# Attention and a gated feed-forward layer on one core: the weight scale from column sums for six steps and from squares for twelve

## The chip, the cores and the metric

The kernel runs on one core of a Trainium2 chip. The metric is device microseconds (us) of one execution. The five engines are named as the profile names them: PE (matrix products), DVE (VectorE), ACT (ScalarE), POOL (GpSimd) and SP (which mostly issues DMAs). Each takes the instructions of its own queue strictly in order.

## The reference

Eight batches of eight heads of causal attention (576 positions, 64 columns) with a bias from cumulative sums, and behind it a gated feed-forward layer over all 4608 positions:

```python
scores = q @ k.T / sqrt(64)
bias   = -(cum[:, None] - cum[None, :])            # cum: running sum of max(s, 0)
scores = where(causal, -1e9, scores + minimum(bias, 0))
attn   = softmax(scores)
x      = (attn @ v)  as  [4608, 512]
gate   = sigmoid(x @ w_gate);  val = x @ w_val     # 512 -> 1536
out    = (gate * val) @ w_out                      # 1536 -> 512
```

All inputs are float32 values held in 64-bit floats; the outputs have to be as accurate as float32 products.

## The kernel before

Products run as sums of float16 products: each operand is scaled by a power of two and split into a high part and a low part, and three of the four part products are added. The first eight heads (NN = 8) are an exception: they are computed in float32 (functions whose names begin with n_), and their instructions are emitted inside `first()`, which raises their priority by 1000 in the scheduler.

The program is emitted in ticks, five to a head (NTL = 5, one for each block of query rows). A tick emits scores (line 489 and 491), masked maxima (529), exponentials (530), the split of the probabilities (534, 539) and the products with v (562 to 564) of neighbouring heads, and, from tick 44 on (NE), units of the feed-forward layer. A unit (g, f) takes 256 positions and 128 of the 1536 hidden columns: `ffn_in` (24 products at line 714, tanh at 719, the gate at 721), `ffn_mid` (the split of the hidden values, 729 and 730) and `ffn_out` (products at 744). The first two groups, g = 0 and 1, run all 24 of their `ffn_in` first, then `hidden_scale`, which needs the scales of all weights, and only then their `ffn_out`.

The weights come in 18 steps. Steps 0 to 11 each bring 128 columns of w_gate and w_val, steps 12 to 17 each 256 rows of w_out. A step is `load_weight` (DMA, lines 279 and 286, most of them issued from ACT's queue), `decode_weight` (64-bit to 32-bit: one ACT and three DVE operations on 128x1024, lines 298 to 301), the scale, and `split_weight` (high part on ACT, line 337, low part on DVE, line 338). The rooms into which raw and decoded weights go are borrowed: ws and wa are their own, w2all is the future w_out, t2f the gates of the first two groups, io the output rows. Step n can be loaded when the step that last used its room is through. Steps 0 to 5 are emitted in ticks below 40, during the float32 heads; steps 6 to 17 from tick 44 on, by `emit_unit`'s neighbours in the loop, so that a unit's weights are ready three units ahead.

For the scale, `column_bound` multiplies the upper 16 bits of the decoded magnitudes (read as bfloat16) by a matrix of ones: eight products at line 310 into one bank, a maximum over them on DVE (313), and two small integer operations (332, 334) that make a power of two of it. The else branch for weights that aren't 64-bit (`m is None`) exists already and isn't used: a Square with a running sum on ACT (326), a sum over the partitions on POOL (328), and the two small operations of `pow2_of` (148, 150).

The order on each engine is set when the program is built: a scheduler takes the emitted instructions, their dependences, priorities and modelled costs and writes down one sequence for each engine. `keep_in_program_order` pins a few loads.

Of the kernel before, what the change touches and what calls it, by code (L numbers as in the profile page):

```python
# [10 lines left out]
F32 = mybir.dt.float32  # L11
F32R = mybir.dt.float32r
I32 = mybir.dt.int32
I64 = mybir.dt.int64
AF = mybir.ActivationFunctionType
ALU = mybir.AluOpType
ADD_REDUCE = bass.bass_isa.ReduceOp.add

P = 128
# [6 lines left out]
def tile_attention_then_gated_ffn(  # L26
# [11 lines left out]
    nc = tc.nc  # L38
# [11 lines left out]
    NTL = len(TILES)  # L50
# [4 lines left out]
    NN = H  # L55
# [7 lines left out]
    pp = ctx.enter_context(tc.tile_pool(name="pp", bufs=2, space=bass.MemoryType.PSUM))  # L63
# [69 lines left out]
    wscale = cp.tile([P, 2, NF], F32, name="wscale")  # L133
# [8 lines left out]
    def first(now=True):  # L142
        return tc.high_priority(1000) if now else ExitStack()

    def pow2_of(dst, ss, tag):

        e = wp.tile([P, 1], I32, tag="xe", name=f"xe_{tag}")
        nc.vector.tensor_scalar(e, ss.bitcast(I32), 1, 0x3F800000, ALU.logical_shift_right, ALU.bitwise_and)
        n = dst.shape[1]
        nc.vector.tensor_scalar(dst.bitcast(I32), e.to_broadcast([P, n]) if n > 1 else e, -1.0, 204.0 * 2.0 ** 23,  # L150
                                ALU.mult, ALU.add)
# [72 lines left out]

    wide = w_gate.dtype == I64
    wst, wdec, wtot = {}, {}, {}

    rows_out = cp.tile([P, 2 * DM], F32, name="io")
    t2big = cp.tile([P, 2 * NF * GT], F32, name="t2f")
# [23 lines left out]
    def room(n):  # L253

        o, f = wsteps[n]
        if o == 0:
            return raw[f % 3], dec[f % 3], n - 3
        i, j, last = outroom[f // 2]
        return raw[i], dec[j], last
# [30 lines left out]
    def decode_weight(n):  # L290

        o, f = wsteps[n]
        r, a, _ = room(n)
        if not wide:
            return a.bitcast(F32), None
        m = w2all[:, f // 2].rearrange("p l h x n -> p (l h x n)") if o else w1[f].rearrange("p c g l n -> p (c g l n)")
        m = m.bitcast(I32)
        nc.scalar.activation(a.bitcast(F32), r[:, :, 1].bitcast(F32), AF.Copy, scale=2.0 ** -112)
        nc.vector.tensor_scalar(m, a, 3, 0x7FFFFFF8, ALU.logical_shift_left, ALU.bitwise_and)
        nc.vector.scalar_tensor_tensor(a, a, -0x80000000, m, ALU.bitwise_and, ALU.bitwise_or)  # L300
        nc.vector.scalar_tensor_tensor(a, r[:, :, 0], 29, a, ALU.logical_shift_right, ALU.bitwise_or)
        return a.bitcast(F32), m

    def column_bound(n, m):

        top = m.bitcast(BF16).rearrange("p (n t) -> p n t", t=2)[:, :, 1]
        early = wnext["tick"] < NTL * NN
        ps = pp.tile([P, 512], F32, tag="av" if early else "o", name=f"wps{n}", **({"bufs": 1} if early else {}))
        for c in range(8):
            nc.tensor.matmul(ps[:, :P], ones, top[:, c * P : (c + 1) * P], start=c == 0, stop=c == 7)  # L310
        tot = wp.tile([P, 1], F32, tag="wst", name=f"wtot{n}")
        junk = lp.tile([P, P], BF16, tag="wj", name=f"wj{n}")
        nc.vector.tensor_scalar(junk, ps[:, :P], 2.0 ** -100, None, ALU.max, ALU.max, accum_out=tot)
        return tot

    def split_weight(n, a, m):

        o, f = wsteps[n]
        if o:
            hi, lo = (w2all[:, f // 2, l].rearrange("p h x n -> p (h x n)") for l in range(2))  # L320
        else:
            a = a.rearrange("p (c n) -> p c n", n=P)
            hi, lo = (w1[f].rearrange("p c g l n -> p (c g) l n")[:, :, l] for l in range(2))
        if m is None:
            ss = wp.tile([P, 1], F32, tag="wss", name=f"wss{n}")
            nc.scalar.activation(hi, a, AF.Square, accum_out=ss)
            tot = wp.tile([P, 1], F32, tag="wst", name=f"wtot{n}")
            nc.gpsimd.partition_all_reduce(tot, ss, P, ADD_REDUCE)
            pow2_of(wscale[:, o, f : f + 1 + o], tot, f"w{n}")
        else:  # L330
            e = wp.tile([P, 1], I32, tag="xe", name=f"xe_w{n}")
            nc.vector.tensor_scalar(e, column_bound(n, m).bitcast(I32), 0x7F800000, None, ALU.bitwise_and)
            dst = wscale[:, o, f : f + 1 + o]
            nc.vector.tensor_scalar(dst.bitcast(I32), e.to_broadcast([P, 2]) if o else e, -1.0, 268.0 * 2.0 ** 23,
                                    ALU.mult, ALU.add)
        sc = wscale[:, o, f : f + 1]
        nc.scalar.activation(hi, a, AF.Copy, scale=sc)
        nc.vector.scalar_tensor_tensor(lo, a, sc, hi, ALU.mult, ALU.subtract)
# [21 lines left out]
        osc[b] = wp.tile([P, 1], F32, tag="osc", name=f"osc{b}", bufs=3)  # L360
        nc.vector.tensor_scalar(osc[b], gmax, sv[b][1], 2.0 ** 14, ALU.mult, ALU.mult)

    wnext = {"load": 0, "step": 0, "tick": 0}

    def weight_step():
        n = wnext["step"]
        while n and wnext["load"] < len(wsteps) and room(wnext["load"])[2] < n:
            if not NF <= wnext["load"] < NF + 2:
                load_weight(wnext["load"])
            wnext["load"] += 1  # L370
        split_weight(n, *decode_weight(n))
        wnext["step"] = n + 1
# [426 lines left out]
    for n in range(nticks + 12):  # L799
        if n == NTL * EARLY:  # L800
            more_room()
        i, t = divmod(n, NTL)
        wnext["tick"] = n
        if i < NN:
            with first():
                n_s(i, NTL - 1 - t)
# [7 lines left out]
        if 2 <= n < nticks + 2:  # L814
            a, z = divmod(n - 2, NTL)
# [5 lines left out]
        if 1 <= n < nticks + 1:  # L821
            a, z = divmod(n - 1, NTL)
# [7 lines left out]
        if 3 <= n < 3 + NTL * NN:  # L830
            with first():
                a, z = divmod(n - 3, NTL)
# [113 lines left out]
        if n >= NE and state["u"] < 2 * NF:  # L946
            fdone = min(NF, int((n - NE + 1) * FPT))
            while state["u"] < 2 * fdone:
                f = state["u"]
# [17 lines left out]
        m = n - (11 if n > 2 * NTL * H + 30 else 7)  # L967
# [42 lines left out]
```

## Time and profile before

| | |
|---|---|
| median of 3 runs | 1151.53 us (1150.67 to 1153.77) |
| profiled execution, its own time | 1150.28 us |
| its span | 1148.5 us |
| granted TensorE clock, mean | 0.993 |
| PE busy | 1096.8 us, 96% |
| DVE, ACT, POOL busy | 756.4, 733.5, 199.9 us |

All durations below are from the one profiled execution; the time outside its span is 1.78 us. Rows of the profile name line, engine, operation, output <- input and the shape; a row that begins with a number gives start and duration in us, and in square brackets how long the engine had been idle before it and what it waited for. A table by windows gives for each stretch its length, each engine's busy time with the number of instructions, the granted clock, the busy share of the DMA engines and their rate. A row of waits gives the total in us, how often, and the longest.

### The profile page before, as it was taken

Reading aid. Unit: us, or ns where it says so; the run is one execution under the profiler, and the core shown is the slowest. Engines: PE = TensorE matmul, PEld = TensorE weight load, DVE = VectorE, ACT = ScalarE, POOL = GpSimd, SP = SyncE. Lnnn points to the kernel's source line nnn. Section 1 sums busy time; section 2 is a strip of 40 time slices with the busy share of each in tenths; the row PEclk is TensorE's granted clock in tenths of the full one; section 3 lists DMA queues with packets and bytes.
Section 4 is the critical chain, followed back from the end, with each engine's and each line's share of the span. In section 5 each row is a group of like instructions: output and inputs, shape, how many; then the busy total and the mean of one; then the engine's idle time right before and its main releaser. Section 6 shows DMA issues by size and latency. Waiting matters only on the chain.

```text
span 1148.5 us, 30266 instructions
## 1 busy us (share of the span) xinstructions
PE 1096.8 (96%) x11868; PEld 861.6 (75%) x11868; DVE 756.4 (66%) x2212; ACT 733.5 (64%) x1437; POOL 199.9 (17%) x473
## 2 busy tenths in 40 slices
PE   6998878999999999999999999999999999999998
PEld 4776757757777887788777777778877787787775
DVE  6868989876787777665565667777777775222222
ACT  5869667867776777676665667778676765233222
POOL 3301101022232222121211122212221211000000
PEclk9999999999999999999999999999999999999999
DMA  9766986997989688866645488878787774000000
GB/s 282 218 189 140 181 178 144 174 200 154 178 159 187 150 186 158 154 139 135 148 87 130 90 175 163 170 144 175 152 159 146 142 123 88 13 20 20 1 19 19
DMA packets 445517, 157.63 MB, mean 137 GB/s; under 512 B 403583, under 2 KB 435839, under 8 KB 445374
## 3 DMA queue, kind: packets, MB, share of 16 engines
q1 hardware_dynamic: 418686, 127.38, 56.7%
q10 hardware_dynamic: 23328, 17.04, 4.9%
q0 software_dynamic: 3360, 11.27, 2.8%
q8 instruction: 93, 1.52, 0.6%
q14 instruction: 50, 0.41, 0.1%
HBM read 56.92 MB, written 9.58 MB: 58 GB/s over the span
## 4 chain that ended last, share of the span: by engine, by line
PE 72%; DMA 10%; DVE 6%; issue 5%; ACT 3%; SPq 3%; POOL 1%; ACTq 0%; DVEq 0%; POOLq 0%
PE gv L714 39%; PE o L744 21%; DMA v<-in_v_dram 3%; PE s L491 3%; PE s L489 2%; DMA T<-qk 2%; PE na_ps L662 1%; SPq L463 1%; DVE e L529 1%; PE av L564 1%; PE av L562 1%; PE av L563 1%; DMA qk<-in_q_dram 1%; DMA w2all<-in_moe_w_out_dram 1%; PE s L631 1%
## 5 line engine op out<-in xcount | busy, mean ns | idle before, releaser
L714 PE MATMUL gv<-x,w 128*128 128x256 f16 (+3 forms) x6912 | 619.2, 247 | 10.1 <-DVE t2f L721 9.1
L714 PEld LDWEIGHTS <-w 128*128 128x128 f16 x6912 | 536.0, 98 | 75.0 <-issue 11.5
L744 PE MATMUL o<-w2all,h 128*128 128x512 f16 x1296 | 313.7, 379 | 1.8 <-ACT h L729 1.8
L530 ACT ACTIVATE e<-e,em 128x576 f32<-128x576 f32 x280 | 153.2, 556 | 92.5 <-DVE em L529 89.8
L744 PEld LDWEIGHTS <-h 128*128 128x128 f16 x1296 | 123.3, 98 | 109.1 <-ACT h L729 2.1
L719 ACT ACTIVATE th<-gv,scb 128x256 f32<-128x256 f32 (+3 forms) x288 | 110.8, 410 | 138.6 <-PE gv L714 130.5
L721 DVE SCALAR_TENSOR_TENSOR t<-th,gv 128x256 f32<-128x256 f32 x192 | 80.0, 417 | 147.9 <-ACT th L719 146.8
L511 POOL TENSOR_SCALAR_AFFINE_SELECT rl<-rl 128x128 f32<-128x128 f32 (+1 forms) x240 | 85.8, 358 | 503.1 <-DVE em L529 462.3
L529 DVE CUSTOM_DVE_ANT_0 e<-s,rl,qkcf 128x576 f32<-128x576 f32 x280 | 151.5, 545 | 31.7 <-PE s L491 15.6
L729 ACT ACTIVATE h<-t,hsc 128x256 f16<-128x256 f32 x192 | 96.7, 504 | 92.4 <-DVE t L721 92.4
L539 DVE SCALAR_TENSOR_TENSOR p<-e,p 128x384 f16<-128x384 f32 x224 | 103.1, 500 | 45.1 <-ACT p L534 44.3
L730 DVE SCALAR_TENSOR_TENSOR h<-t,hsc,h 128x256 f16<-128x256 f32 x192 | 93.7, 488 | 44.9 <-ACT h L729 42.6
L534 ACT ACTIVATE p<-e 128x1152 f16<-128x1152 f32 x112 | 111.9, 1000 | 2.7
L489 PE MATMUL s<-T 128*128 128x288 f16 (+2 forms) x246 | 64.1, 278 | 7.8 <-DVE em L529 4.0
L562 PE MATMUL av<-v,pt 128*128 128x65 f16 x560 | 67.7, 193 | 2.2 <-DMA pt<-p 2.2
L451 POOL PARTITION_BROADCAST cr<-cr x63 | 59.4, 947 | 56.0 <-DMA cr<-cum_d 42.0
L563 PE MATMUL av<-v,pt 128*128 128x64 f16 x560 | 67.7, 192 | 0.0
L564 PE MATMUL av<-v,pt 128*128 128x65 f16 x560 | 67.6, 194 | 0.0
L491 PE MATMUL s<-T 128*128 128x288 f16 (+2 forms) x246 | 61.5, 277 | 4.0 <-DMA T<-T 3.9
L562 PEld LDWEIGHTS <-pt 128*128 128x128 f16 x560 | 52.5, 97 | 7.9 <-DMA pt<-p 3.1
L563 PEld LDWEIGHTS <-pt 128*128 128x128 f16 x560 | 52.5, 97 | 4.5
L564 PEld LDWEIGHTS <-pt 128*128 128x128 f16 x560 | 52.7, 97 | 0.2
(164 smaller groups left out, 1297.0 us busy)
## 6 DMA issues: line engine op xcount, KB each, us to landing
v<-v SPq DMA_DIRECT2D x56, 162.5 KB
out_dram<-io POOLq DMA_DIRECT2D x34, 256.0 KB, 3.2
v<-in_v_dram SPq DMA_DIRECT2D x64, 128.0 KB
T<-T SPq DMA_DIRECT2D x82, 72.0 KB
t2f<-in_v_dram SPq DMA_DIRECT2D x20, 288.0 KB
qk<-in_q_dram SPq DMA_DIRECT2D x17, 288.0 KB
qk<-in_k_dram SPq DMA_DIRECT2D x17, 288.0 KB
w2all<-in_moe_w_gate_dram ACTq DMA_DIRECT2D x7, 512.0 KB
```

What stands on the lines that cost most here:

```text
L491: nc.tensor.matmul(ps[:, : b_ - a], lhs, T[i][:, 2, a:b_], start=False, stop=not mask)
L529: nc.vector.tensor_tensor_reduce(e, ps, r, c, MASKED, ALU.add, ALU.min, acc)
L530: nc.scalar.activation(e_t[t][:, :w], e_t[t][:, :w], AF.Exp, bias=acc, scale=-1.0)
L534: nc.scalar.activation(p_s[h_][:, 0], e_s[h_], AF.Copy, scale=PSCALE)
L539: nc.vector.scalar_tensor_tensor(flat[:, LOW[t] * P : (LOW[t] + t) * P], e_t[t][:, : t * P], PSCALE, flat[:, kb * P : (kb + t) * P], ALU.m ...
L562: nc.tensor.matmul(AV[i][:, t], hi, v_[:, D : 2 * D + 1], start=kb == 0, stop=False)
L563: nc.tensor.matmul(AV[i][:, t, 0:D], hi, v_[:, 0:D], start=False, stop=False)
L564: nc.tensor.matmul(AV[i][:, t], lo, v_[:, D : 2 * D + 1], start=False, stop=False)
L714: nc.tensor.matmul(ps[:, gv, a:e], w1[f][:, cc, gv, wl], x_of(b, cc)[:, xl, c0 + a : c0 + e], start=(c == 0), stop=(c == 3 * NC - 1))
L719: nc.scalar.activation(th[:, a:e], ps[:, 0, a:e], AF.Tanh, scale=scb[b][:, f : f + 1])
L729: nc.scalar.activation(h[:, 0], t2, AF.Copy, scale=hsc[:, f : f + 1])
L744: nc.tensor.matmul(ps[:m], h[:, hl, tt * P : tt * P + m], w2[f][:, wl], start=(f == 0 and c == 0), stop=(f == NF - 1 and c == 2))
```

## The change

Steps 0 to 5 keep the column sums; their products, maximum and small operations are emitted inside `first()`, with the priority of the float32 heads. Steps 6 to 17 return no magnitudes from `decode_weight`, and so take the branch with Square, the sum over the partitions and `pow2_of`. The count of ticks that chose the bank of the column sums goes.

```diff
     wst, wdec, wtot = {}, {}, {}
+    NSUM = 6
...
-        return a.bitcast(F32), m
+        return a.bitcast(F32), m if n < NSUM else None
...
-        early = wnext["tick"] < NTL * NN
-        ps = pp.tile([P, 512], F32, tag="av" if early else "o", name=f"wps{n}", **({"bufs": 1} if early else {}))
+        ps = pp.tile([P, 512], F32, tag="av", name=f"wps{n}", bufs=1)
...
             e = wp.tile([P, 1], I32, tag="xe", name=f"xe_w{n}")
-            nc.vector.tensor_scalar(e, column_bound(n, m).bitcast(I32), 0x7F800000, None, ALU.bitwise_and)
-            dst = wscale[:, o, f : f + 1 + o]
-            nc.vector.tensor_scalar(dst.bitcast(I32), e.to_broadcast([P, 2]) if o else e, -1.0, 268.0 * 2.0 ** 23,
-                                    ALU.mult, ALU.add)
+            with first():
+                nc.vector.tensor_scalar(e, column_bound(n, m).bitcast(I32), 0x7F800000, None, ALU.bitwise_and)
+                dst = wscale[:, o, f : f + 1 + o]
+                nc.vector.tensor_scalar(dst.bitcast(I32), e.to_broadcast([P, 2]) if o else e, -1.0, 268.0 * 2.0 ** 23,
+                                        ALU.mult, ALU.add)
...
-    wnext = {"load": 0, "step": 0, "tick": 0}
+    wnext = {"load": 0, "step": 0}
...
-        wnext["tick"] = n
```

Line numbers of the changed kernel are one higher from line 227 on, the same from 307 to 331, and again one higher from 332. The scheduler writes another order with it. Three places show how. In the rows below a name such as em8_3 is the maximum of head 8, block 3, w1_6 the parts of weight step 6, th0_9 the tanh of unit (0, 9), and the number behind a last underscore is the scheduler's.

DVE at the masked maxima of the first float16 head, head 8, before:

```order
L529 ISA e_1_80,em8_3_1215<-s8_3_1196,rl8_1167,qkcf4_1055 128x448
L529 ISA em8_3_1215 128x1
L334 TENSOR_SCALAR wscale_118<-xe_w5_1019 128x1
L154 TENSOR_SCALAR invw_117<-wscale_118 128x3
L377 TENSOR_SCALAR scb0_1272<-invw_117,vin0_340 128x3
L529 ISA e_0_79,em8_2_1248<-s8_2_1211,rl8_1167,qkcf4_1055 128x320
```

and after the change:

```order
L530 ISA e_1_80,em8_3_1215<-s8_3_1196,rl8_1167,qkcf4_1055 128x448
L530 ISA em8_3_1215 128x1
L339 SCALAR_TENSOR_TENSOR w1_5_71<-w2all_78,wscale_118,w1_5_71 128x8x128
L339 SCALAR_TENSOR_TENSOR w1_6_72<-wa0_147,wscale_118,w1_6_72 128x8x128
L530 ISA e_0_79,em8_2_1248<-s8_2_1211,rl8_1167,qkcf4_1055 128x320
L530 ISA em8_2_1248 128x1
L339 SCALAR_TENSOR_TENSOR w1_7_73<-w2all_78,wscale_118,w1_7_73 128x8x128
```

The low parts of steps 5, 6 and 7 have moved in between the maxima; the last small operation of step 5 has moved ahead of them.

ACT at the loads of w_out into t2f (step 16) and w2all (step 15), before:

```order
L719 ACTIVATE th0_8_1735<-gv0_8_1710,scb0_1272 128x256
L279 DMA t2f_145<-in_moe_w_out_dram 128x8x128
L286 DMA t2f_145<-in_moe_w_out_dram 128x8x128
L337 ACTIVATE w2all_78<-io_144,wscale_118 128x1024
L502 ACTIVATE rl12_2784<-cr12_2678,qkcf6_2664 128x576
L502 ACTIVATE rl13_2915<-cr13_2795,qkcf6_2664 128x576
L279 DMA w2all_78<-in_moe_w_out_dram 128x8x128
L286 DMA w2all_78<-in_moe_w_out_dram 128x8x128
L719 ACTIVATE th0_9_1765<-gv0_9_1740,scb0_1272 128x256
```

and after the change, with the rows between the two loads left out:

```order
L326 ACTIVATE w2all_78,wss12_1645<-io_144 128x1024
L326 ACTIVATE w2all_78,wss13_1784<-wa0_147 128x1024
L280 DMA t2f_145<-in_moe_w_out_dram 128x8x128
L720 ACTIVATE th0_6_1550<-gv0_6_1525,scb0_1272 128x256
L287 DMA t2f_145<-in_moe_w_out_dram 128x8x128
...
L431 ACTIVATE qk16_13_2707<-qk32_6_2166,qksc6_2566 96x6x64
L280 DMA w2all_78<-in_moe_w_out_dram 128x8x128
L287 DMA w2all_78<-in_moe_w_out_dram 128x8x128
L720 ACTIVATE th0_9_1709<-gv0_9_1684,scb0_1272 128x256
```

The load into t2f stands two tanh earlier, 20 rows ahead of the load into w2all instead of 5.

PE at the first output products (o0_0 and o0_1), before:

```order
L714 LDWEIGHTS w1_10_76
L714 MATMUL gv1_10_2321<-x3_142,w1_10_76 128x256
L744 LDWEIGHTS h0_0_2388
L744 MATMUL o0_0_2391<-w2all_78,h0_0_2388 128x512
...
L744 MATMUL o0_1_2395<-w2all_78,h0_0_2388 128x512
L714 LDWEIGHTS w1_11_77
L714 MATMUL gv1_11_2349<-x0_139,w1_11_77 128x256
```

and after the change:

```order
L715 LDWEIGHTS w1_8_74
L715 MATMUL gv1_8_2169<-x3_142,w1_8_74 128x256
L745 LDWEIGHTS h0_0_2292
L745 MATMUL o0_0_2295<-w2all_78,h0_0_2292 128x512
...
L745 MATMUL o0_1_2299<-w2all_78,h0_3_2321 128x512
L715 LDWEIGHTS w1_9_75
L715 MATMUL gv1_9_2197<-x0_139,w1_9_75 128x256
```

The output products have moved ahead of the units (1, 9) and (1, 10), and four hidden columns' worth of them stand together.

## The prediction

> **What bounds the kernel now.** I read the page's totals and slices first, then a table of the stretches in which weight steps 6 to 17 run, then the waits in them.
>
> ```profile
> span 1148.5 us, 30266 instructions
> PE 1096.8 (96%) x11868; PEld 861.6 (75%) x11868; DVE 756.4 (66%) x2212; ACT 733.5 (64%) x1437; POOL 199.9 (17%) x473
> PE   6998878999999999999999999999999999999998
> DVE  6868989876787777665565667777777775222222
> ACT  5869667867776777676665667778676765233222
> ```
>
> PE is busy for 1096.8 of 1148.5 us, so 51.7 us are idle. The slices (28.7 us each) say where: PE stands below 9 in slices 0 and 3 to 6 and at the very end, and from slice 7 (201 us) on it is full. A kernel of that kind ends when PE's work has passed through; time is won only by less PE work, or by less PE idleness in the first 270 us. The table cuts that part where the stages change.
>
> ```profile
> core 0: us, PE busy (x) PEld busy (x) DVE busy (x) ACT busy (x) POOL busy (x), PEclk, DMA share, GB/s
> 85.00:110.00 25.00, 22.35 (x198) 18.79 (x198) 20.39 (x72) 23.18 (x46) 5.26 (x8) 1.00 0.71 148
> 110.00:158.00 48.00, 37.17 (x416) 31.39 (x417) 47.11 (x125) 34.07 (x55) 4.02 (x5) 0.93 0.78 152
> 158.00:170.00 12.00, 7.27 (x49) 5.50 (x49) 8.03 (x21) 6.53 (x10) 0.00 (x0) 0.86 1.17 243
> 170.00:218.00 48.00, 41.93 (x485) 36.18 (x482) 44.68 (x134) 35.22 (x64) 6.26 (x9) 1.00 0.82 167
> 218.00:246.00 28.00, 25.84 (x241) 15.64 (x242) 22.97 (x72) 22.56 (x48) 4.30 (x12) 1.00 0.88 168
> 246.00:270.00 24.00, 23.51 (x218) 14.66 (x218) 15.11 (x41) 15.46 (x29) 7.16 (x14) 1.00 0.71 170
> 270.00:345.00 75.00, 71.58 (x926) 57.70 (x924) 58.30 (x178) 56.91 (x119) 20.15 (x44) 1.00 0.89 169
> ```
>
> From 110 to 218 us DVE is the bound, not PE: it is busy for 47.11 of 48 us, then for 44.68 of 48, while PE idles for 10.8 and 6.1 us and ACT for 13.9 and 12.8. Only 158 to 170 is different: there all three idle. The stage ends at the first output product, which needs the hidden scale, and so all 18 weight steps:
>
> ```profile
> 217.58 1.69 ACT L729 ACTIVATE h<-t2f,hsc 128x256 f16<-128x256 f32 x4
> 218.13 1.04 PE L744 MATMUL o<-w2all,h 128*128 128x512 f16 x4 [1.78 <-ACT h L729]
> ```
>
> **Part one: twelve column sums go from PE and DVE.** The prices:
>
> ```profile
> 131.01 1.07 PE L310 MATMUL wps<-w,ones 128*128 128x128 bf16 x16
> 131.92 2.78 PE L714 MATMUL gv<-x,w 128*128 128x256 f16 x24
> 134.54 0.19 PE L562 MATMUL av<-v,pt 128*128 128x65 f16 x1
> 134.57 0.19 PE L563 MATMUL av<-v,pt 128*128 128x64 f16 x1
> L313 DVE TENSOR_SCALAR_CACHE_REDUCE wj<-wps x18: 252/278/292, 16.0 to 198.1; 128x128 bf16<-128x128 f32 x18
> L313 DVE DVE_READ_ACCUMULATOR wj<-wps x18: 75/80/85, 16.2 to 198.3; 128x1 f32 x18
> ```
>
> The first row holds the column sums of two steps; PE starts its next work 131.92 - 131.01 = 0.91 us later, so a step is 0.455 us and twelve are 5.5 us of PE. On DVE the maximum gives way to its accumulator read 0.2 us after its start (16.0 to 16.2, and again 198.1 to 198.3), and the read takes 0.08: 0.28 a step, 3.4 us for twelve. The two small integer operations of a step stay two of the same shape, at no cost. All of this lies between 92 and 200 us, where PE has idle time anyway, so the 5.5 us don't come off the end by themselves.
>
> **Part two: twelve squares on ACT.** No square of this size is in the trace. From below I bound it by the scaled copy of the same 128x1024 float32 input alone, from above by that copy with a whole accumulator read behind it:
>
> ```profile
> L337 ACT ACTIVATE w<-w2all,wscale x8: 1132/1137/1160, 24.4 to 150.8; 128x1024 f16<-128x1024 f32 x8
> L403 ACT ACTIVATION_READ_ACCUMULATOR jq<-qk x34: 185/187/193, 84.2 to 880.4; 96x1 f32 x34
> ```
>
> That is 12 x 1.137 = 13.6 to 12 x 1.324 = 15.9 us; I take 15, since reads behind an instruction on ACT partly overlap it. ACT has 133 - 99.0 = 34.0 us idle from 85 to 218 by the table, which is the cover. If it were gone, the 15 us would stand in front of the tanh and exps that DVE waits for. Where a square stands between a decode and the scaled copy of its own step, DVE has other work in its queue.
>
> **Part three: twelve all-reduces on POOL.** The size differs little: a 96-row or 128-row sum of one column.
>
> ```profile
> L406 POOL PARTITION_ALL_REDUCE qkt<-ssq x28: 403/408/1214, 86.3 to 910.9; - x28
> L451 POOL PARTITION_BROADCAST cr<-cr x63: 855/856/2292, 22.6 to 944.2; - x63
> ```
>
> 12 x 0.41 = 4.9 us on an engine that is busy for 15.5 of the 133 us from 85 to 218, so its own time costs nothing. But DVE's small operations of a step now wait for square, all-reduce and whatever POOL has ahead (a broadcast of 0.86 us, or a memset that waits for a product), and DVE's queue is strictly in order: behind them stand the exp masks and scores' maxima of the running head. I put new waits on DVE at +1.0 us between 0 (each step has another DVE instruction ahead) and 4 (every third of twelve steps waits a whole all-reduce behind a broadcast, 1.0 us).
>
> POOL and DVE also meet. One decode in the trace coincided with a broadcast:
>
> ```profile
> L301 DVE SCALAR_TENSOR_TENSOR w2all<-w2all x8: 1209/1218/1627, 18.8 to 138.9; 128x1024 int32<-128x1024 int32 x8
> L301 DVE SCALAR_TENSOR_TENSOR wa<-w2all,wa x1: 1681/1681/1681, 176.4 to 176.4; 128x1024 int32<-128x1024 int32 x1
> 176.33 2.52 POOL L451 PARTITION_BROADCAST cr<-cr  x2
> ```
>
> The same form took 1.681 instead of 1.218, so a collision costs 0.46 us. Between 0 and all twelve reduces colliding, 0 to 5.5 us; I take 0.5, one collision, since an all-reduce lasts half a broadcast. [...]
>
> **Part four: what the order does with it.** Up to about 65 us the orders are identical; the priority reaches steps 0 to 5 alone and moves only step 5's small operations by a few rows. From the second FFN unit of the second group (270 us) PE's order is again the same apart from swaps of neighbours, so what happens lies between. Three things follow from the rows of the order shown with the change.
>
> First, the stores of low halves of steps 6 and 7 now stand between head 8's masked scores on DVE, where DVE waited. Second, the w_out load into w2all, whose issue blocked ACT, is now issued elsewhere: the other load stands some 11 us of work ahead of it. The waits:
>
> ```profile
> DVE e L529 <- PE s L518: 2.9, 3, 1.5
> DVE t2f L721 <- ACT th L719: 1.5, 1, 1.5
> DVE x L689 <- ACT x L688: 0.7, 1, 0.7
> DVE w2all L338 <- ACT w2all L337: 0.6, 1, 0.6
> DVE w2all L299 <- ACT io L298: 0.4, 1, 0.4
> 158.69 3.98 ACTq L286 DMA_DIRECT2D w2all<-in_moe_w_out_dram  x1
> 162.77 0.47 ACT L719 ACTIVATE th<-gv,scb 128x256 f32<-128x256 f32 x1 [2.88 <-issue]
> ```
>
> The fill takes 0.7 + 1.5 = 2.2 us. The issue of 3.98 us held ACT's tanh for 2.88 us, and DVE behind it for 1.5 + 0.6 + 0.4 = 2.5 us. DVE's work ahead of the first hidden half is otherwise equal (203.7 before, 204.1 after, adding the durations of the trace before over the rows of either order): the 3.4 us saved go to attention work of heads 14 and 17 that has come ahead of it. So the first output product moves by -2.2 - 2.5 + 1.0 + 0.5 = -3.2, from 218.1 to about 215 us.
>
> Third, PE has done less by then. The first output product followed gate-and-value unit gv1_10 and now follows gv1_8; units 9 and 10 of the second group stand behind it. A unit is 134.54 - 131.92 = 2.62 us, two are 5.2. Against that 40 attention products at 0.03 us each (134.54 to 134.57), 1.2 us, are now ahead. PE's work left at the first output product grows by 4.0 us. In other words: most of the 5.5 us taken from PE shortens a stage that DVE ends.
>
> Behind the first product PE idles for 2.2 us up to 246 and 0.5 up to 270 by the table, and waits for
>
> ```profile
> PE av L562 <- DMA pt<-p: 1.9, 2, 1.1
> PE gv L714 <- DMA x<-x: 0.6, 1, 0.6
> ```
>
> These are transposes and inputs that arrive by DMA, 2.5 us. With 4.0 us more of independent work ahead of the consumers, each of the two waits of up to 1.1 us can be covered; I leave the one about 1.1 us long and take away the rest: -1.4. From 270 us on I count nothing, since the order is the same.
>
> **The sum.** -3.2 (first product earlier) + 4.0 (more PE work behind it) - 1.4 (less idle) = -0.6 us. The profiled execution took 1150.28 us, 1.78 more than its span and 1.25 less than the median of the three runs, 1151.53. 1150.28 - 0.6 = 1149.7, and on the median's scale 1150.9 us: no change that could be measured. I call 0.3%, 3.45 us, the bound of that: 1148.1 to 1155.0.
>
> **The rivals.** *The saved PE work comes off whole.* If DVE's stage shrinks by its own 3.4 us on top of the filled waits, or PE uses idle places so that the two units don't stand behind, the end moves by PE's 5.5 us: 1150.28 - 5.5 + 1.25 = 1146.0. For it: PE idles for only 2.7 of the 52 us from 218 to 270 and 3.4 of 75 after, so any work less at 218 is time. Against it: 21.6 us of PE idleness lie at 110 to 218, and this is where the work goes. It decides itself at the first output product: before 212 us with two units behind, or 215 with none.
>
> *The first product does not come forward.* If new waits for the all-reduces (4.0 in place of 1.0) use up the fills, the start of the output product stays at 218, the two units still stand behind it and nothing of the 1.4 comes: +4.0, 1150.28 + 4.0 + 1.25 = 1155.5. For it: ACT is busy for 23.18 of 25 us from 85 to 110, where the square of step 7 and the scaled copies of steps 6 and 7 are added. It decides from new DVE waits of 4 us up.
>
> *POOL locks DVE.* If each all-reduce costs DVE as the broadcast did, 12 x 0.46 = 5.5 us in the DVE-bound stretch, less the 0.5 in the sum: 1150.9 + 5.0 = 1155.9. Against it: POOL is busy for 4.02 of 48 us in the densest DVE stretch with no mark on DVE's rate, and 8 decodes have a median of 1.218.
>
> *The change does nothing:* the prioritised steps 0 to 5 hardly move, but the other twelve certainly do; I give this no chance of its own, and its time is inside the forecast's.
>
> **How the numbers follow.** The forecast 0.43; PE's 5.5 us come off whole 0.28, and further gains (the waits vanish and units fit in) 0.05; first product not forward 0.14; POOL locks DVE 0.10. Faster 0.33, same 0.43, slower 0.24. The range goes past 1146.0 by half the PE idle time of 270 to 345 us (1.7) to 1144.3, and past 1155.9 by half of the 3.0 us that part three's waits may lie over the value taken, to 1157.4; the likeliest case alone has 1148.1 to 1155.0.
>
> **What would show it.** The column-sum products go from 144 to 48; twelve squares of about 1.14 us and twelve all-reduces of 0.41 appear. The first output product starts at about 215 us, two gate-and-value units follow it that had preceded, and the load into w2all is issued in about 0.7 us rather than 3.98. Two-input decodes remain near 1.22 us. DVE's waits in 85 to 170 us are smaller by about 4 us. The prediction is wrong if the first product starts before 212 or after 218, if PE's idle time after 218 changes by more than 2 us, or if a decode of 128x1024 takes 1.6 us regularly.

## The result and the profile after

The changed kernel takes 1162.12 us (median of 6 runs, 1158.27 to 1163.33); the kernel before, run beside it, 1152.17 us (6 runs, 1150.67 to 1155.94). The ratio is 1.0084, with a 95% interval from 1.0063 to 1.0105: slower by some 10 us, where no measurable change was forecast. The profiled execution of the changed kernel has a span of 1159.9 us against 1148.5. The head of its page and PE's slices:

```profile
span 1159.9 us, 30094 instructions
...
PE 1097.6 (95%) x11772; PEld 859.5 (74%) x11772; DVE 757.1 (65%) x2188; ACT 746.3 (64%) x1461; POOL 208.7 (18%) x485
...
PE   6887777899899999999999999999999999999998
...
PEclk9998899899999999999999999999999999999999
```

PE issues 96 products less, as the diff says, and yet is busy for longer, 1097.6 us against 1096.8. Idle it is for 1159.9 - 1097.6 = 62.3 us against 51.7. So the 11.4 us of span are 10.6 of idle PE and 0.8 of busy PE. By the price in the prediction the busy time should have fallen by 5.5 us; instead it was stretched by 5.5 + 0.8 = 6.3. The row PEclk says by what: its tenths fall to 8 in three slices, where the kernel before has 9 in all, and the mean granted clock is 0.984 against 0.993. The granted clock and PE's rows confirm the sum: with PE's busy time at half clock counted half, PE's work is 1089.6 us before and 1084.1 after, 5.5 less; what half clock adds is 7.2 us before and 13.5 after, 6.3 more. The rows show what half clock does to a product: those of line 715 on 128x256 start 109 ns apart from 141.14 us on, at a clock of 1.00, and 213 ns apart from 208.71 us on, at 0.50.

Where it happens, in windows of the same times, before and then after the change (columns: length; busy time of PE, PE's weight loads, DVE, ACT, POOL; granted clock, DMA share, GB/s):

```profile
65.00:110.00 45.00, 40.33 (x335) 33.49 (x334) 31.26 (x105) 37.44 (x75) 7.30 (x12) 1.00 0.72 172
110.00:158.00 48.00, 37.17 (x416) 31.39 (x417) 47.11 (x125) 34.07 (x55) 4.02 (x5) 0.93 0.78 152
158.00:218.00 60.00, 49.20 (x532) 41.69 (x531) 52.71 (x155) 41.74 (x73) 6.26 (x9) 0.97 0.89 183
218.00:285.00 67.00, 64.35 (x678) 42.79 (x679) 48.76 (x146) 49.38 (x102) 14.21 (x34) 1.00 0.82 169
285.00:430.00 145.00, 140.52 (x1799) 112.93 (x1798) 110.82 (x333) 106.82 (x218) 35.66 (x82) 1.00 0.85 171
```

```profile
65.00:110.00 45.00, 39.02 (x296) 31.49 (x295) 29.73 (x94) 38.13 (x73) 8.26 (x13) 0.96 0.66 161
110.00:158.00 48.00, 33.82 (x348) 27.89 (x347) 45.70 (x118) 38.99 (x67) 7.47 (x12) 0.86 0.80 170
158.00:218.00 60.00, 45.40 (x507) 37.36 (x507) 54.57 (x154) 48.31 (x83) 11.09 (x14) 0.94 0.93 170
218.00:285.00 67.00, 64.50 (x610) 43.67 (x611) 43.02 (x123) 45.67 (x96) 13.33 (x28) 1.00 0.77 167
285.00:430.00 145.00, 138.39 (x1714) 110.97 (x1713) 108.24 (x329) 103.53 (x211) 33.87 (x80) 0.98 0.82 162
```

Between 65 and 285 us PE idles for 37.3 us instead of 29.0, and between 285 and 430 for 6.6 instead of 4.5. The longest of PE's waits from 65 to 285 us, five before and then four after:

```profile
PE gv L714 <- DVE t2f L721: 9.1, 6, 3.3
PE s L491 <- DMA T<-T: 3.9, 4, 1.9
PE s L489 <- DMA T<-qk: 3.7, 3, 2.4
PE nx_ps L686 <- DVE x L689: 3.4, 1, 3.4
PE av L562 <- DMA pt<-p: 2.2, 3, 1.1
```

```profile
PE av L563 <- DMA pt<-p: 13.3, 6, 4.3
PE s L490 <- DVE em L530: 5.2, 4, 2.0
PE gv L715 <- ACT x L689: 4.0, 1, 4.0
PE gv L715 <- DVE t2f L722: 3.9, 4, 1.7
```

The waits are not only longer, they are others. The wait for the gate on DVE has shrunk from 9.1 to 3.9 us. In its place PE stands before attention products whose transposed probabilities (pt) have not arrived, for 13.3 us instead of 2.2. In the traces of both kernels the rows of PE (11868 and 11772), DVE (2212 and 2188) and ACT (1437 and 1461) run in the written order, line by line, and in PE's order gate products stand behind these. That these could have run is not shown for all; the first one behind the longest of these waits (4.3 us, up to 127.41 us) starts at 128.22 us without a wait of its own.

The hidden scale came later too. The last decode, the last small operation and the hidden scale on DVE, before (the prediction shows the first hidden half and output product):

```profile
200.94 1.21 DVE L301 SCALAR_TENSOR_TENSOR wa<-ws,wa 128x1024 int32<-128x1024 int32 x1
204.28 0.15 DVE L334 TENSOR_SCALAR wscale<-xe_w 128x2 int32<-128x2 int32 x1
213.50 0.23 DVE L354 TENSOR_SCALAR hsc<-hsg,hsr 128x12 f32<-128x12 f32 x1
```

and after, with the squares, ACT's wait, the first hidden half and the output product:

```profile
204.75 1.21 DVE L302 SCALAR_TENSOR_TENSOR wa<-ws,wa 128x1024 int32<-128x1024 int32 x1
205.65 1.04 ACT L326 ACTIVATE w2all<-io 128x1024 f16<-128x1024 f32 x1
206.69 1.04 ACT L326 ACTIVATE w2all<-wa 128x1024 f16<-128x1024 f32 x1
210.37 0.22 DVE L150 TENSOR_SCALAR wscale<-xe_w 128x2 int32<-128x2 int32 x2
217.43 0.22 DVE L355 TENSOR_SCALAR hsc<-hsg,hsr 128x12 f32<-128x12 f32 x1
219.80 0.61 ACT L429 ACTIVATE qk<-qk,qksc 96x384 f16<-96x384 f32 x1 [3.00 <-DMA T<-qk]
220.83 1.69 ACT L730 ACTIVATE h<-t2f,hsc 128x256 f16<-128x256 f32 x4
222.77 4.91 PE L745 MATMUL o<-w2all,h 128*128 128x512 f16 x22
```

From the end of the last decode to the last scale it is 4.6 us instead of 2.3 (210.37 + 0.22 less 205.96; 204.43 less 202.15), the decode ends 3.8 us later, and the first hidden half stands behind the split of head 17, for which ACT waits 3.00 us. The first output product starts at 222.77 us; before it was 218.13, and 215 was forecast.

### The profile page after: what moved, and what is told of

It is laid out like the page before. It is cut to its first block, busy times and chain, and to the rows that moved or that the text cites. A ratio compares the mean times of both kernels' runs of the same rounds, so it can differ in the third digit from the quotient of the medians.

```text
span 1159.9 us, 30094 instructions
## 1 busy us (share of the span) xinstructions
PE 1097.6 (95%) x11772; PEld 859.5 (74%) x11772; DVE 757.1 (65%) x2188; ACT 746.3 (64%) x1461; POOL 208.7 (18%) x485
## 4 chain that ended last, share of the span: by engine, by line
PE 68%; DMA 10%; issue 8%; DVE 6%; ACT 5%; POOL 2%; SPq 2%; ACTq 0%; POOLq 0%; DVEq 0%
PE gv L715 36%; PE o L745 19%; DMA v<-in_v_dram 4%; PE s L492 2%; PE s L490 2%; DMA pt<-p 2%; PE na_ps L663 1%; PE s L632 1%; POOL rl L512 1%; PE av L563 1%; PE av L565 1%; PE av L564 1%; SPq L464 1%; DVE e L530 1%; DMA T<-qk 1%
## 5 line engine op out<-in xcount | busy, mean ns | idle before, releaser
L563 PE MATMUL av<-v,pt 128*128 128x65 f16 x560 | 68.3, 193 | 14.4 <-DMA pt<-p 13.3
L452 POOL PARTITION_BROADCAST cr<-cr x63 | 61.7, 982 | 47.9 <-DMA cr<-cum_d 34.7
```

The costliest lines, as they stand in the source:

```text
L563: nc.tensor.matmul(AV[i][:, t], hi, v_[:, D : 2 * D + 1], start=kb == 0, stop=False)
```

## The experiments

Ratios are to the kernel before on the same chip, whose median was 1150.14 to 1151.16 us in these comparisons. Three theories were tried first: that the longer way of the last scales is the cause (late scale), that the load on ACT and POOL is (load, square or lock theory), and that the changed order is, whatever changed it (order theory). The order theory's ranges are wide, and a time inside them says little; what bears on it are the kernels in which nothing but the order differs.

**The priority alone.** All 18 steps keep the column sums:

```diff
-        return a.bitcast(F32), m if n < NSUM else None
+        return a.bitcast(F32), m
...
-            with first():
+            with first(n < NSUM):
```

> All 18 steps keep the column sums; only the priority of steps 0 to 5 is taken from the change. Late-scale theory (the longer way of the scale of the last w_out steps, over ACT, POOL and DVE, holds up the hidden scale and with it the first output product): no square, so no change, 1152 us, first output product at 218 us. Load theory (fifteen us of squares on ACT and twelve reduces on POOL cost time where DVE and ACT are near full): also 1152. Order theory (any rearrangement of the rows before 270 us shifts the end by up to 10 us, whatever it is): only step 5's small rows move, 1149 to 1155. If it is above 1157, the priority is the cause and all three are wrong.

1150.45 us, ratio 1.0011 (0.9996 to 1.0025): no change. The order of all four engines is the one before, row for row; the priority moves nothing, not even step 5's operations. Whatever the change does comes from its other part: the squares, the longer way of the scale and the column sums that go.

**Half of the squares.** Squares in steps 6 to 11 alone (`m if n < NSUM or n >= NF else None`):

> Squares for steps 6 to 11 only (gate and value weights), column sums for the six w_out steps. Late-scale theory: the w_out scales are ready as before, so the first output product stays within 2 us of 218 and the whole within 2 us of 1152. Load theory: half of the squares, half of the loss, 1157. Order theory: anything from 1147 to 1162.

and in steps 12 to 17 alone (`m if n < NF else None`):

> Squares for the six w_out steps only, column sums for steps 0 to 11. Late-scale theory: the whole loss, 1159 to 1163, first output product at 222 us or later. Load theory: half of the loss, 1157. Order theory: anything from 1147 to 1162.

1157.76 us, ratio 1.0069 (1.0041 to 1.0098), and 1158.55 us, 1.0066 (1.0039 to 1.0094). Either half loses most of what both lose: the parts don't add up. The late scale alone would have left the first half at no loss, so as the only cause it falls. In the second run the first output product starts at 219.2 us, close to before, and the loss is there all the same.

**The load beside the column sums.** The kernel before, with squares and reduces for steps 6 to 17 whose results nothing uses:

```diff
+        if n >= 6:
+            ss = wp.tile([P, 1], F32, tag="wss", name=f"wss{n}")
+            nc.scalar.activation(hi, a, AF.Square, accum_out=ss)
+            jt = wp.tile([P, 1], F32, tag="wjt", name=f"wjt{n}")
+            nc.gpsimd.partition_all_reduce(jt, ss, P, ADD_REDUCE)
         sc = wscale[:, o, f : f + 1]
```

> The kernel before with all its column sums, and beside them, for steps 6 to 17, the same squares and the same sums over the partitions, whose results nothing uses. Late-scale theory: the scale does not wait for them, though each scaled copy stands behind its square on ACT; a loss of 2 to 6 us, 1154 to 1158, and the first output product at 219 to 222. Load theory: the whole load and none of the savings on PE and DVE, 1162 to 1170. Order theory: anything.

1157.47 us, ratio 1.0057 (1.0032 to 1.0083). Less than the load theory's 1162, although nothing is saved on PE and DVE. The scheduler had written another order here as well, so load and order are not parted by it. The first output product starts at 215.2 us, ahead of before: the loss does not depend on it.

**POOL alone.** The reduce of the same size behind the column sum, result unused, without the square:

```diff
+        if n >= 6:
+            jt = wp.tile([P, 1], F32, tag="wjt", name=f"wjt{n}")
+            nc.gpsimd.partition_all_reduce(jt, tot, P, ADD_REDUCE)
```

> The kernel before, and beside its column sums twelve sums over the partitions on POOL for steps 6 to 17, whose results nothing uses. The order of PE, DVE and ACT is that of the kernel before, row for row; only POOL has twelve rows more. It prices POOL alone. Lock theory (a reduce shuts DVE out): 12 x 0.4 to 0.5 us in the DVE-bound stretch, 1156 to 1157, with the decodes of lines 300 and 301 at 1.6 us or more where a reduce runs. Order theory: within 2 us of 1151.

1152.38 us, ratio 1.0010 (0.9985 to 1.0034). The window of the dense DVE stretch, and the decode's rows:

```profile
110.00:158.00 48.00, 38.96 (x423) 32.20 (x421) 47.56 (x132) 34.92 (x57) 15.79 (x12) 0.89 0.71 152
L301 DVE SCALAR_TENSOR_TENSOR w2all<-w2all x8: 1214/1218/1627, 19.4 to 140.6; 128x1024 int32<-128x1024 int32 x8
```

POOL is busy there for 15.79 us instead of 4.02, and the decode's median is 1.218 us as before. Over the whole kernel one decode takes more than 1.3 us (1.627 at 53.8 us), where the kernel before has two. The lock theory falls. If the meeting costs time, the trace has it on POOL, whose durations are rough: the twelve reduces take 0.38 to 3.49 us here, with a median of 1.29, against a median of 0.42 in the changed kernel.

**Another order with the same work.** Three kernels have column sums in all 18 steps and the same number of instructions on PE, DVE, ACT and POOL as the kernel before. The priority on the sums and small operations of steps 12 to 17:

```diff
+            with first(n >= NF):
                 nc.vector.tensor_scalar(e, column_bound(n, m).bitcast(I32), 0x7F800000, None, ALU.bitwise_and)
                 ...
```

> Nothing is added or taken away against the kernel before: only the small operations and column sums of the six w_out steps get the priority of the float32 heads, and the scheduler writes another order (first output product behind 20 gate-and-value units instead of 23). Order theory (the order of the kernel before was a good one among many, and any other interleaving of attention and feed-forward before 270 us loses 5 to 12 us): 1156 to 1162. Square theory (the squares' time on ACT and the longer way of the scale cost the time): 1148 to 1153, since there is no square in it.

the same on all 18 steps (`with first():`):

> As the kernel before, with the priority on the column sums and small operations of all 18 steps; the first output product stands behind 23 units, and behind 280 attention products as in the changed kernel, instead of 240. Order theory: 1156 to 1162, and PE waits of 10 us or more for transposed probabilities, as in the changed kernel. Square theory: 1148 to 1153.

and the bank of the attention products for the late column sums (`early = True`):

> As the kernel before, with the column sums of the late steps in the bank of the attention products too; the order changes most of all (22 units, but only 80 attention products ahead of the first output product). Order theory: 1156 to 1165. Square theory: 1148 to 1154, with a loss only where column sums wait for the bank.

1155.93 us, ratio 1.0049 (1.0034 to 1.0064); 1156.40 us, 1.0059 (1.0037 to 1.0082); 1163.95 us, 1.0115 (1.0087 to 1.0143). Without a square, a reduce or a longer way of any scale, another order alone loses more than half of what the change did in the first two kernels. The third loses more than the change, but it isn't order alone: its late column sums share a bank with the attention products, and PE waits 3.6 us for the maximum over them (65 to 285 us). The first of the three, by its page, its first output product and three of the waits of PE from 65 to 285 us:

```profile
span 1155.3 us, 30262 instructions
...
PE 1102.1 (95%) x11868; PEld 865.7 (75%) x11868; DVE 758.9 (66%) x2212; ACT 734.5 (64%) x1437; POOL 204.1 (18%) x473
...
216.12 1.04 PE L745 MATMUL o<-w2all,h 128*128 128x512 f16 x4 [0.80 <-ACT h L730]
PE gv L715 <- DVE t2f L722: 8.5, 6, 2.1
PE s L490 <- DMA T<-qk: 7.2, 3, 3.5
PE av L563 <- DMA pt<-p: 4.0, 4, 1.3
```

The count of PE's instructions is that of before, 11868. Its first output product starts 2.0 us ahead of before, and still the kernel is slower: PE's busy time has grown by 5.3 us, at a mean clock of 0.987. The expected 10 us of waits for transposed probabilities in the second kernel were only 4.1; there PE waited 9.5 us for the transposed queries and keys instead. So no single wait is common to the bad orders.

**Squares in other orders.** The priority on the whole of the last six steps:

```diff
-        split_weight(n, *decode_weight(n))
+        with first(n >= NF):
+            split_weight(n, *decode_weight(n))
```

> The changed kernel with the priority of the float32 heads on the whole of the last six weight steps (decode, square, reduce, split). The work is that of the changed kernel; the order puts the first output product behind 23 units and 280 attention products. Order theory: no rule says where it lands, 1148 to 1164; like the orders tried so far most likely 1155 to 1162. Square theory (the squares cost what the changed kernel lost, whatever the order): 1159 to 1163. Late-scale theory: the scales of the last steps come earlier, so 1152 to 1156.

1161.28 us, ratio 1.0086 (1.0070 to 1.0103): no remedy. Next, the number of column sums (NSUM; the priority stays on the first six steps, and later column sums go into the bank of before):

> The changed kernel with squares from step 3 on instead of 6: three more column sums (1.4 us of PE) go, three more squares come. The order becomes very different: the first output product stands behind 11 units and 160 attention products. Square theory: 15 squares in place of 12, 1162 to 1166. Order theory: not bound to the number of squares, 1150 to 1170.

> The changed kernel with column sums for steps 0 to 8 and squares for 9 to 17 (without the priority on steps 6 to 8). First output product behind 21 units and 240 attention products. Square theory: 9 of 12 squares, three quarters of the loss, 1158 to 1160. Order theory: 1148 to 1164.

> Squares for steps 7 to 17 (11), column sums for 0 to 6. First output product behind 24 units and 305 attention products. Cost per square (0.8 us each, from the changed kernel's 10 us for 12): 1160. Order alone: not bound to the number, 1149 to 1166, and by the attention that runs furthest ahead rather at 1158 to 1164.

> Squares for steps 10 to 17 (8). First output product behind 22 units and 265 attention products. Cost per square: 1157 to 1158, above the run with nine squares only by noise. Order alone: 1149 to 1164, with no relation to the 1152 of the neighbour with nine squares.

> Squares for steps 11 to 17 (7). First output product behind 22 units and 240 attention products. Cost per square: 1157. Order alone: 1149 to 1164.

> Squares for steps 15 to 17 (3), the last three steps. The place of the first output product is that of the kernel before, though 760 rows of PE's order differ. Late-scale theory: the hidden scale comes later by the longer way, first output product at 221 us or later, 1155 to 1159. Cost per square: 1153 to 1154. Order alone: nearest to the kernel before, so 1150 to 1155, with PE waits of 26 to 31 us between 65 and 285 us (28.7 before).

And no bound at all in twelve steps, with a constant instead:

```diff
-            nc.scalar.activation(hi, a, AF.Square, accum_out=ss)
...
-            pow2_of(wscale[:, o, f : f + 1 + o], tot, f"w{n}")
+            nc.vector.memset(wscale[:, o, f : f + 1 + o], 2.0 ** 13)
```

> Leaves the weight scale of steps 6 to 17 out: a constant 2^13 written by a small memset takes the place of square, reduce and small operations. No column sum, no square, no reduce in 12 steps, and no dependence of the scale on the data; the first output product stands behind 4 units only. Square theory: the work is smaller than in either kernel, 1143 to 1148 (1151 less PE's 5.5 us and part of DVE's 3.4). Order theory: another order like any, so 1148 to 1165 in spite of less work.

All of them in one table, sorted by PE's idle time from 65 to 285 us, which is the sum of length less busy time over windows like those above:

| kernel | squares | PE idle 65 to 285, us | mean clock | median, us | ratio (95%) |
|---|---|---|---|---|---|
| unused reduces | 0 | 26.3 | 0.989 | 1152.38 | 1.0010 (0.9985 to 1.0034) |
| squares from 9 | 9 | 28.7 | 0.986 | 1151.83 | 1.0020 (0.9999 to 1.0042) |
| priority alone | 0 | 28.9 | 0.991 | 1150.45 | 1.0011 (0.9996 to 1.0025) |
| squares from 3 | 15 | 28.9 | 0.975 | 1166.75 | 1.0134 (1.0111 to 1.0157) |
| before | 0 | 29.0 | 0.993 | | 1 |
| squares from 15 | 3 | 29.9 | 0.988 | 1152.37 | 1.0023 (1.0008 to 1.0037) |
| squares from 11 | 7 | 30.5 | 0.992 | 1150.48 | 1.0004 (0.9986 to 1.0022) |
| column sums, priority 12 to 17 | 0 | 31.5 | 0.987 | 1155.93 | 1.0049 (1.0034 to 1.0064) |
| unused squares and reduces | 12 | 31.8 | 0.989 | 1157.47 | 1.0057 (1.0032 to 1.0083) |
| fixed scale | 0 | 32.6 | 0.984 | 1156.30 | 1.0039 (1.0026 to 1.0053) |
| squares 12 to 17 | 6 | 33.1 | 0.986 | 1158.55 | 1.0066 (1.0039 to 1.0094) |
| column sums, priority on all | 0 | 33.8 | 0.984 | 1156.40 | 1.0059 (1.0037 to 1.0082) |
| squares, whole steps with priority | 12 | 34.5 | 0.984 | 1161.28 | 1.0086 (1.0070 to 1.0103) |
| squares 6 to 11 | 6 | 34.7 | 0.985 | 1157.76 | 1.0069 (1.0041 to 1.0098) |
| squares from 10 | 8 | 34.8 | 0.986 | 1156.89 | 1.0070 (1.0046 to 1.0095) |
| the change (squares from 6) | 12 | 37.3 | 0.984 | 1162.12 | 1.0084 (1.0063 to 1.0105) |
| column sums, one bank | 0 | 38.2 | 0.983 | 1163.95 | 1.0115 (1.0087 to 1.0143) |
| squares from 7 | 11 | 40.3 | 0.981 | 1158.65 | 1.0080 (1.0049 to 1.0110) |

Nine squares lose nothing measurable, eight lose 0.7%, seven nothing, six in the last steps 0.66%: kernels that differ by one square differ by 0.5 to 0.66%, and not in the order of their number. The fixed scale, with the least work, is slower than before. What sorts the table is how long PE stands from 65 to 285 us: up to 30.5 us of idle time nothing or 0.23% is lost, from 31.5 on at least 0.39%, with one exception, squares from 3, whose clock is the lowest. The line between 30.5 and 31.5 is finer than one trace can draw: three kernels with the same rows on PE (before, priority alone, unused reduces) have 29.0, 28.9 and 26.3 us. And idle time is a part of the time it is set against, so the table tells where the time is lost and not why. The exception, by its page:

```profile
PE 1105.5 (95%) x11748; PEld 866.0 (74%) x11748; DVE 756.4 (65%) x2182; ACT 750.0 (65%) x1467; POOL 208.0 (18%) x488
```

It has the fewest products of all in PE's queue, 11748, and the longest busy time, 1105.5 us. Counted from 0 to 285 us, idle time and what half clock adds come to 66.8 us there (45.9 and 20.9), the most of all. Before, priority alone, unused reduces and squares from 11 have 48.9 to 51.6 us by this count, squares from 7 and one bank 66.4 and 66.2, and the others, which lose 0.20 to 0.86%, 55.6 to 60.9. So with the two kinds of lost time together squares from 3 is no exception. The order theory stands: order alone is enough for a loss of 0.5 to 0.6%. A small price of the squares themselves is not excluded by these runs: the four kernels with ten or more squares that are used are all slower by 0.8% or more, and an order without loss was not found for them. None of the sixteen kernels is faster than the one before by more than its interval.

## Why the prediction was wrong

**What bounds the kernel.** Right for the end (PE is full from 430 us on in both) and for the stretch (DVE is busy for 45.70 of 48 us from 110 to 158 after the change too).

**Part one.** The 96 products are gone, but PE's busy time did not fall. The price was right, 5.5 us at full clock; half clock, which the prediction did not count, took 6.3 us in its place. The accumulated maximum was gone as said.

**Part two.** The square takes 1.04 us from start to start (205.65 to 206.69 us, the accumulator read of 0.19 overlapping it and the next one), so twelve are 12.5 us, below the lower bound of 13.6. ACT's busy time rose by 746.3 - 733.5 = 12.8 us. The size was off by a sixth, and it is not what failed.

**Part three.** The reduce has its 0.4 us (a median of 0.418), and the lock did not come. Two decodes take more than 1.3 us after the change (1.628 and 1.743 us) as before it (1.627 and 1.681), and the one of 1.743 us ran beside a broadcast (1.09 us from 129.49 us on), not a reduce: the 0.5 us for a collision with a reduce did not come either. What failed is the new-waits term, +1.0 us with bounds of 0 and 4. It was built from the waits of the added instructions on DVE. The new waits are on PE, for data of attention that the order had moved: +11.1 us for the transposed probabilities alone, less 5.2 at the gate, and with the others +8.3 us of idle PE from 65 to 285 us.

**Part four, the fills.** They came. The low halves of steps 5 and 6 run between head 8's maxima without a gap, and the load into w2all is issued in 0.58 us instead of 3.98:

```profile
101.81 0.68 DVE L530 CUSTOM_DVE_ANT_0 e<-s,rl,qkcf 128x448 f32<-128x448 f32 x1
102.42 1.28 DVE L339 SCALAR_TENSOR_TENSOR w<-w2all,wscale,w 128x1024 f16<-128x1024 f32 x1
103.61 1.28 DVE L339 SCALAR_TENSOR_TENSOR w<-wa,wscale,w 128x1024 f16<-128x1024 f32 x1
161.26 0.58 ACTq L287 DMA_DIRECT2D w2all<-in_moe_w_out_dram  x1
```

They did not bring the first product forward, since other waits opened behind them. DVE's waits from 85 to 170 us were to shrink by about 4 us; they are 8.3 us instead of 7.7, and the largest is new, 2.9 us for attention products: PE stands until 127.41 us for their transposed probabilities, and DVE behind it until 128.44. At 222.77 us the first product missed the forecast of 215 by 7.8. And the step from there to the end failed as well: the sum has +4.0 - 1.4 = +2.6 us behind the first product, and the span grew by 11.4 - 4.6 = 6.8. Its form failed too: the experiments have first output products from 145.7 us (fixed scale) to 237.6 (squares from 7), and the two slowest kernels, squares from 3 and one bank, have theirs at 189.2 and 203.7, ahead of before. So the marker on which the sum hung tells little of the end. What goes with it is PE's lost time up to 285 us.

**From 270 us on, nothing.** Wrong by 4.8 of the 11.4 us. Matched by their number, the attention products lag behind those of before by 6.9 us at 286 us and by 11.7 at 419. The last jump is at 410: DVE stands behind a split of v that waits for its load, a score product waits 2.17 us for a maximum, and then the clock halves (rows below). The order was the same there: from 352.7 us on (345.5 before) PE's rows are those of before, one for one. So equal rows lose time too when what they wait for comes at other times, and the same order behind a change does not mean the same time.

**The priority.** The sentence that it moves step 5's operations by a few rows is refuted: alone it moves none.

**The rivals.** The whole gain of PE's work did not come, and POOL locks nothing. The rival on the slow side, that the first product does not come forward, was nearest: its place was right (new waits eat the fills), but its price of 4.0 us was less than half, its waits were sought on DVE behind the reduces, and its 1155.5 us lie 6.6 below the measured median. The range ended at 1157.4 because all new waits were priced from the kernel before, whose order happens to have few of them; a change of order had no term of its own.

## What to carry to other kernels

Where a scheduler writes the order and the kernel's order is already a good one, price any edit that moves rows by a few equal-work reorderings run beside it: here two of them cost 0.49 and 0.59%, as much as the 5.5 us (0.48%) of PE work that the edit saved. Rows that have moved ahead bring their own waits, and what stands behind them waits too: here PE stood 4.30 us for one DMA, up to 127.41 us, and the gate product behind it started at 128.22 us without a wait of its own. Judge such a change by the bounding engine's lost time up to the point where it is full, idle time and reduced clock together, and not by the start of one marked instruction.

## What the runs showed of the hardware that was not expected

After some of PE's waits its granted clock fell to 0.50, and this adds to what idle time costs. The wait at 410 us in the changed kernel, then two microseconds each behind it:

```profile
412.64 0.28 PE L490 MATMUL s<-T 128*128 128x288 f16 x1 [2.17 <-DVE em L530]
410.47:412.64 2.17, 0.00 (x1) 0.00 (x0) 1.93 (x6) 2.17 (x7) 0.72 (x2) 1.00 0.96 219
412.64:414.64 2.00, 2.00 (x23) 1.89 (x23) 0.65 (x4) 1.97 (x8) 0.29 (x2) 0.74 0.82 190
414.64:416.64 2.00, 2.00 (x22) 2.00 (x20) 2.00 (x6) 1.79 (x3) 1.13 (x2) 0.50 1.14 289
416.64:418.64 2.00, 2.00 (x15) 1.20 (x14) 1.58 (x5) 0.85 (x3) 0.49 (x2) 0.90 0.59 138
418.64:420.64 2.00, 2.00 (x51) 1.83 (x50) 1.48 (x6) 1.19 (x3) 0.48 (x1) 1.00 0.95 169
```

After 2.17 us without a product PE runs at half clock for parts of three windows: 0.52 + 1.00 + 0.20 = 1.7 us are lost to the clock, nearly as much again as the wait. Not each wait does so: others of 1.95 and 2.69 us in the same trace (up to 145.88 and 219.83 us) are followed by a full clock. In this trace and that of the kernel before, ten stretches at 0.50 lie ahead of PE's last product, seven here and three there: six are 3.41 us long, three 6.83 and one 10.24, and in each trace their starts are whole multiples of 3.41 us apart. Counted on in steps of that length, the wait of 2.17 us fell whole into one, with PE busy for 1.24 us of it; the one of 2.69 was split over two, with 1.50 and 2.64; the one of 1.95 lies in one but for 0.03 us, with 1.49:

```profile
410.20:413.61 3.41, 1.24 (x18) 1.01 (x16) 2.47 (x8) 3.41 (x9) 1.02 (x3) 1.00 0.89 204
413.61:417.03 3.42, 3.42 (x36) 3.42 (x34) 2.74 (x8) 2.79 (x8) 1.32 (x2) 0.50 1.04 258
143.96:147.37 3.41, 1.49 (x14) 1.33 (x15) 3.41 (x10) 2.54 (x6) 0.56 (x1) 1.00 0.50 108
147.37:150.78 3.41, 3.41 (x32) 2.92 (x31) 3.41 (x9) 3.38 (x8) 0.38 (x1) 1.00 0.60 112
215.64:219.06 3.42, 1.50 (x14) 1.09 (x12) 2.98 (x12) 1.14 (x3) 0.00 (x0) 1.00 0.75 158
219.06:222.47 3.41, 2.64 (x24) 2.29 (x25) 2.02 (x5) 2.67 (x7) 0.00 (x0) 1.00 1.08 224
```

So here a wait of 2.17 us drew half clock behind it and one of 2.69 did not. In the steps just ahead of the ten stretches PE was busy for 0.00, 0.79, 1.18, 1.24, 1.46, 1.79 and 1.92 us here and for 0.98, 1.11 and 1.73 us in the kernel before. The larger of these lie beside the 1.49 and 1.50 that a full clock followed, so the busy time of one step does not settle it, and what does was not shown.

The clock also differs between executions of one order: the kernels before, with the priority alone and with unused reduces have the same rows on PE and 0.993, 0.991 and 0.989, with PE busy for 1096.8, 1098.5 and 1099.7 us. How much of the changed kernel's loss is clock and how much is waiting was worked out from one execution (6.3 and 10.6 us, against 5.5 saved) and not tried apart by a run. Why the order of the kernel before waits so little stays open too, and so does why the attention products' data came late in the changed order.
